# An attention, expert and mixer kernel: shared token differences, and unread matmuls beside batch 0's attention

## The chip, the cores and the metric

The kernel runs on one core of one Trainium2 chip. The metric is the device time of one execution in microseconds, the median of the runs. A core has TensorE (PE, matmuls), VectorE (DVE), ScalarE (ACT), GpSimd (POOL) and SyncE (SP, which here issues most DMAs), each with its own instruction stream executed in order.

## What is computed

Three stages, one after another, on 4 batches of 576 tokens with 512 channels (8 heads of 64):

```python
# attention, with a bias from a running sum of s
scores = scale * q @ k.T + min(-(cum[i] - cum[j]), 0), causal
x = softmax(scores) @ v                       # 4 x 576 x 512
# gated expert ("MoE"), with token mixtures
x_prev = x shifted by one token, zero first
xk = mu_k * x + (1 - mu_k) * x_prev
xr = mu_r * x + (1 - mu_r) * x_prev
y = sigmoid(xr @ w_r) * (relu(xk @ w_k) ** 2 @ w_v)
# mixer
u = y + (relu(y.T @ w_tok1) @ w_tok2).T
out = u + relu(u @ w_ch1) @ w_ch2
```

The weights arrive in 64-bit floats and are turned into pairs of 32-bit values (a high and a low part) on the chip; most products are then three matmuls (high by high, high by low, low by high).

## The kernel before

**Order.** The program is written with a tile framework: each piece of work is given a place (`at(x)`), a planner orders the instructions of each engine by place and by its own estimate of durations, and the semaphores follow from the tiles. An edit therefore can change the order of instructions that it doesn't touch. Buffers come from pools; a tile waits for the release of an older one of the same tag. `ps_d` has two PSUM buffers of tag `d`, used by the expert's products while attention runs.

**Batch 0's attention** is done in two parts. `early(h, j)` (L308) handles the first 256 tokens of head h in two blocks j of 128 queries: a score matmul in fp32 (L314), `softmax_max` (DVE, L258) and `softmax` (exponent on ACT, L268; sum and reciprocal on DVE, L269 and L270; scaling on POOL, L271), transposes on PE (L322), a copy by ACT, and the products with v (`pv`, L332). `late(h, j)` (L354) handles the remaining queries of head h in three blocks, j = 2, 3, 4 (the last of 64 queries), with scores at L364, transposes at L373, and `late_pv(h)` (L381, matmuls at L391) once per head; every second head the result is copied by DVE to `xt` (L393, by the helper at L77). Meanwhile the weights of the expert are loaded by SP (L553) and split by `weight_split` (ACT L75 and L565, DVE L566 and L567, then POOL or DVE L571). The buffers XK, XR and KK lie where the first weights' staging buffers were, so they can't be written before the last of these splits.

**The other batches** use `scores`, `transposes` and `values` (matmuls at L283, L284, L405, L457), 40 blocks per batch.

**The expert** works in chunks of 256 and 320 tokens (`CHS`), two per batch b. Its units (`moe_units`, L518) are laid out beside the attention blocks: per chunk eight `up` units (tile h, L482), then `gate` (tile r) and `down` (tile vd) units, twenty in all. `mix(b, c, i, p)` (L466) makes one 128-channel quarter p of XK (i = 0, read by `up`) or XR (i = 1, read by `gate`): on DVE a TENSOR_SCALAR by mu (L472) and a SCALAR_TENSOR_TENSOR by 1 - mu (L473), a rounding copy on ACT (L474), and the low part on DVE (L475). Its working tile has the tag t, of which there are three, shared with `up`'s. Where the mixtures are made is set at L533 to L540: XR for a first chunk beside its first `up` units, XK for the second chunk of batches 1 to 3 right after the eight `up` units of the first, XR for the second chunk beside the last four units of the first, XK for the next batch's first chunk beside the last units of this batch and the first of the next.

**The mixer** follows when attention is over, from about 500 us on; it is not touched.

The mask tile `maskc` (zeros, and a triangle of large negative values in its last 128 columns) and the identity are made on POOL in `constants` (L146).

Of the kernel before, what the change touches and what calls it, by code (L numbers as in the profile page):

```python
# [8 lines left out]
F32 = mybir.dt.float32  # L9
# [4 lines left out]
AF = mybir.ActivationFunctionType  # L14
ALU = mybir.AluOpType
# [4 lines left out]
def f32(ap):  # L20
    return ap.bitcast(F32)
# [3 lines left out]
def attention_moe_mixer(  # L25
# [16 lines left out]
    nc = tc.nc  # L42
    G, D, _, S = qk.shape
# [6 lines left out]
    KD = DM // 128  # L50
    KF = FF // 128
# [5 lines left out]
    CM = S - QC  # L57
# [6 lines left out]
    def open_pool(**kw):  # L64
        st = ExitStack()
        return st, st.enter_context(tc.tile_pool(**kw))

    def at(place):
        return tc.high_priority(tc.cur_priority - int(place * 1000))
# [3 lines left out]
    def copy(e, out, in_, scale=1.0):  # L73
        if e == "A":
            nc.scalar.activation(out=out, in_=in_, func=AF.Copy, scale=scale)  # L75
        elif e == "D" and scale == 1.0:
            nc.vector.tensor_copy(out, in_)  # L77
        else:
            ENG[e].tensor_scalar(out=out, in0=in_, scalar1=scale, scalar2=1.0, op0=ALU.mult, op1=ALU.mult)

    const = ctx.enter_context(tc.tile_pool(name="const", bufs=1, reuse_waits="tile"))
# [3 lines left out]
    ps_d = ctx.enter_context(tc.tile_pool(name="ps_d", bufs=2, space=PSUM, reuse_waits="tile"))  # L85

    ident = const.tile([128, 128], F32, name="ident")
    maskc = const.tile([128, 512 + 128], BF16, name="maskc")
    mu = const.tile([128, 2, KD], F32, name="mu")
    omu = const.tile([128, 2, KD], F32, name="omu")  # L90

    WK = wp.tile([128, 2 * KD * FF], F32R, name="WK")
    WV = wp.tile([128, 2 * KF * DM], F32R, name="WV")
# [4 lines left out]
    act = {"ps": ps_d}  # L98
# [37 lines left out]
    def pt_tile(slot, dtype=F32):  # L136
        return pt_p.tile([128, (NS - 1) * CM], dtype, tag=f"PT{slot}", name=f"PT{slot}")
# [6 lines left out]
    xt = {}  # L144

    def constants():  # L146
        nc.gpsimd.memset(maskc, 0.0)
        nc.gpsimd.affine_select(
            out=maskc[:, 512:640], in_=maskc[:, 512:640], pattern=[[-1, 128]],
            compare_op=ALU.is_ge, fill=-8.0e9, base=0, channel_multiplier=1,  # L150
        )
        make_identity(nc, ident)

    def mixes():
        for i, m in enumerate((mu_k, mu_r)):
            nc.scalar.dma_start(out=mu[:, i, :], in_=m.rearrange("(k p) -> p k", p=128))
        nc.vector.tensor_scalar(out=omu, in0=mu, scalar1=-1.0, scalar2=1.0, op0=ALU.mult, op1=ALU.add)

# [94 lines left out]
    def softmax_max(j, ps, P, mx, x, c0, c1):  # L255
        m = min(128, S - 128 * j)
        q0 = 128 * j
        nc.vector.tensor_tensor_reduce(  # L258
            out=P[0:m, c0:c1], in0=ps[0:m, 0:c1 - c0], in1=maskc[0:m, 512 - q0 + c0:512 - q0 + c1],
            scale=-scale, scalar=3.0e38 if x == 0 else mx[0:m, x - 1:x],  # L260
            op0=ALU.add, op1=ALU.min, accum_out=mx[0:m, x:x + 1],
        )
# [30 lines left out]
    def early_view(h):  # L293
        t, h0, n = next(x for x in early_at if x[1] <= h < x[1] + x[2])
        return t[:, 0:2 * n * QC].rearrange("p (h t s) -> p h t s", h=n, t=2), h0, n
# [12 lines left out]
    def early(h, j, V0, cp):  # L308
        x, h0, _ = early_view(h)
        w = 128 * j + 128  # L310
        P = cp.tile([128, w], F32, tag=f"E{j}", name=f"P{j}", bufs=2)
        mx = st_p.tile([128, 2], F32, tag="mx", name="mx")
        ps = ps_s.tile([128, 512], F32, tag="s", name="s")
        nc.tensor.matmul(ps[:, 0:w], x[0:D + 2, h - h0, 0, 128 * j:w], x[0:D + 2, h - h0, 1, 0:w], start=True, stop=True)  # L314
        softmax_max(j, ps, P, mx, 0, 0, w)
        softmax(j, P, mx, 0)
        if j == 0:
            pt[0] = ps_t.tile([128, 512], F32, tag="t", name="t")
        ps = pt[0]
        for k in range(j + 1):  # L320
            o = 128 * (j + k)
            nc.tensor.transpose(ps[:, o:o + 128], P[:, 128 * k:128 * k + 128], ident)  # L322
        if j == 0:
            return
        T = cp.tile([128, FIRST], F32, tag="T", name="T", bufs=2)
        copy("A", T, ps[:, 0:FIRST])
        if h % 2 == 0:
            early_ps[h // 2] = ps_v.tile([128, QC], F32, tag="v", name="pv")
        pv = early_ps[h // 2]
        r = slice(D * (h % 2), D * (h % 2) + D)  # L330
        for k in range(2):
            nc.tensor.matmul(pv[r, 128 * k:QC], V0[:, k, h * D:h * D + D], T[:, QC * k:QC + 128 * k], start=k == 0, stop=k == 1)  # L332
        if h % 2 == 1:
            x = xt[0, h // 2] = xt_p.tile([128, 1 + S], F32, tag="xt", name="xt")
            nc.gpsimd.memset(x[:, 0:1], 0.0)
            copy("D", x[:, 1:1 + QC], pv)
# [17 lines left out]
    def late(h, j):  # L354
        m = min(128, S - 128 * j)
        w = 128 * j + m
        q0 = 128 * j
        x = late_x.pop(h) if j == NS - 1 else late_x[h]
        P = p_p.tile([128, w], F32, tag=f"P{j}", name=f"P{j}")
        mx = st_p.tile([128, 2], F32, tag="mx", name="mx")  # L360
        parts = [(0, w)] if w <= 512 else [(0, w // 2), (w // 2, w)]
        for y, (c0, c1) in enumerate(parts):
            ps = ps_s.tile([128, 512], F32, tag="s", name="s")
            nc.tensor.matmul(ps[0:m, 0:c1 - c0], x[0:D + 4, 0, q0:q0 + m], x[0:D + 4, 1, c0:c1], start=True, stop=True)  # L364
            softmax_max(j, ps, P, mx, y, c0, c1)
        softmax(j, P, mx, y)
        if j == QC // 128:
            late_t[h] = pt_tile(h % 2)
        T = late_t[h]
        pt = ps_t.tile([128, 512], F32, tag="t", name="t")  # L370
        for k in range(j + 1):
            r = min(128, S - 128 * k)
            nc.tensor.transpose(pt[0:r, m * k:m * k + m], P[0:m, 128 * k:128 * k + r], ident[0:m, 0:m])  # L373
        o = q0 - QC
        nf = j + 1 if m == 128 else j
        view = T.rearrange("p (k w) -> p k w", w=CM)
        copy("A", view[:, 0:nf, o:o + m], pt[:, 0:m * nf].rearrange("p (k m) -> p k m", m=m))
        if nf <= j:
            copy("A", T[0:TAIL, BLK[j] + o:BLK[j] + o + m], pt[0:TAIL, m * j:m * j + m])
# [83 lines left out]
        nc.scalar.activation(out=tmp[a, 0:n], in_=ps[z, :], func=AF.Copy)  # L463
        nc.vector.tensor_tensor(out=x[a, 1 + base:1 + base + n], in0=ps[a, :], in1=tmp[a, 0:n], op=ALU.add)

    def mix(b, c, i, p):  # L466
        dst = act[("XK", "XR")[i]]
        x = xt[b, p]
        a, z = CHS[c]
        n = z - a  # L470
        t = act["sm"].tile([128, CM], F32, tag="t", name="t", bufs=3)
        nc.vector.tensor_scalar(out=t[:, 0:n], in0=x[:, 1 + a:1 + z], scalar1=mu[:, i, p:p + 1], scalar2=1.0, op0=ALU.mult, op1=ALU.mult)  # L472
        nc.vector.scalar_tensor_tensor(out=t[:, 0:n], in0=x[:, a:z], scalar=omu[:, i, p:p + 1], in1=t[:, 0:n], op0=ALU.mult, op1=ALU.add)  # L473
        nc.scalar.activation(out=dst[:, 0, p, 0:n], in_=t[:, 0:n], func=AF.Copy)  # L474
        nc.vector.tensor_tensor(out=dst[:, 1, p, 0:n], in0=t[:, 0:n], in1=f32(dst[:, 0, p, 0:n]), op=ALU.subtract)  # L475

    def up(b, c, m):
        n = width(c)
# [39 lines left out]
    def moe_units(b):  # L518
        u = []
        for c in range(2):  # L520
            for m in range(KF):
                u.append([(up, b, c, m)])
            seq = [("g", 0), ("g", 1)]
            for m in range(KD):
                seq += [("d", m)] + ([("g", m + 2)] if m + 2 < KD else [])
            for w, m in seq:
                if w == "g":
                    u.append([(gate, b, c, m)])
                else:
                    u.append([(down, b, c, m, 0)])  # L530
                    u.append([(down, b, c, m, 1)])
        n = len(u) // 2
        for p in range(KD):  # L533
            u[1 + p].append((mix, b, 0, 1, p))
            u[KF + 1 + p if b else n - KD + p].append((mix, b, 1, 0, p))
            u[n - KD + p].append((mix, b, 1, 1, p))
            if b + 1 < B and p < KD - 1:
                u[n + n - KD + p].append((mix, b + 1, 0, 0, p))
        if b:
            u[0].insert(0, (mix, b, 0, 0, KD - 1))  # L540
        return u

    def run(acts):
# [51 lines left out]
    def attention_item(n):  # L595
# [65 lines left out]
        with at(N0 + n + 2):  # L661
            if j == QC // 128 - 1:
                values(i, 0)
            if j == NS - 1:
                values(i, 1)

    wst_s, sp = open_pool(name="wst", bufs=5)
    cp_s, cp = open_pool(name="cp", bufs=1)
    cum, e32 = bias_rows(cp)
# [31 lines left out]
    with at(9):  # L701
        mixes()
# [5 lines left out]
    x = 1.0  # L708
# [16 lines left out]
    x = 18  # L725
# [5 lines left out]
            x += 1.5  # L731
    with at(N0):
        for p in range(KD):
            mix(0, 0, 0, p)
    todo = {}
    base = (NS - 2) * H
    starts, ends = [0, 2, 4, 4], [2, 4, 4, 4]
    for b in range(B):
        u = moe_units(b)
        x0 = base + NS * H * (b - 1) + starts[b] if b else 0  # L740
        x1 = base + NS * H * b + ends[b]
        if b == 0:
            x1 = base + NS * H + ends[0]
            u, u1 = u[:len(u) // 2], u[len(u) // 2:]
            for x, acts in enumerate(u1):
                m = base + 1
# [222 lines left out]
```

## Time and profile before

| | |
|---|---|
| three runs | 890.91, 886.45, 890.05 us; median 890.05 |
| profiled execution, whole | 893.86 us |
| its span, first to last instruction | 891.5 us |
| mean granted TensorE clock | 0.965 |
| busy: PE, DVE, ACT, POOL | 94%, 59%, 52%, 35% of the span |
| instructions | 17414 |

The span is that of the execution in which all instructions were recorded; 2.4 us of its time lie around the span. Busy time of PE is from the start of a matmul to its modelled end, so a busy PE need not be at its peak. The granted clock is given as a share of 2.4 GHz; 0.50 is 1.2 GHz.

### The profile page before, as it was taken

The page shows a single profiled execution, that of the slowest core. Times are in us where ns is not written, and L with a number is a line of the kernel's source. Part 1 is how long each engine was busy: PE and PEld are TensorE (multiplying, and loading weights), DVE is VectorE, ACT ScalarE, POOL GpSimd, SP SyncE. Part 2 cuts the span into 40 slices and gives each one's busy share as a digit, 9 for nine tenths or more (in the row PEclk, how much of TensorE's full clock was granted, in tenths as well). Part 3 has the DMA queues.
Part 4 walks back from the last instruction along what each step waited for, and adds up shares of the span by engine and source line. Part 5 has one row for each costly group of instructions (what it writes and reads, how often), then busy time and mean ns, then how long its engine had stood idle before and what let it go on. Part 6 is the DMA issues. An engine that isn't in the chain of part 4 may idle for free.

```text
span 891.5 us, 17414 instructions
## 1 busy us (share of the span) xinstructions
PE 842.4 (94%) x6008; PEld 778.0 (87%) x6008; DVE 523.7 (59%) x1582; ACT 467.3 (52%) x1320; POOL 316.3 (35%) x463
## 2 busy tenths in 40 slices
PE   6578999999889999998999899899999999999998
PEld 4234777998789999888999899899999999999998
DVE  5687786677979677887657866871331322322221
ACT  4685885966786867858546785760320211211210
POOL 4544444754664545645244774650000000000000
PEclk9657999999999999999999999999999999999999
DMA  7972345456646355532042656654021112112100
GB/s 183 202 213 57 99 125 121 109 138 135 155 101 138 82 115 136 128 98 48 20 130 74 189 174 193 208 164 148 25 70 58 46 42 60 43 43 65 43 24 25
DMA packets 74888, 94.19 MB, mean 106 GB/s; under 512 B 10304, under 2 KB 58432, under 8 KB 74800
## 3 DMA queue, kind: packets, MB, share of 16 engines
q1 hardware_dynamic: 68352, 77.40, 33.8%
q0 software_dynamic: 4576, 15.08, 5.5%
q8 instruction: 48, 0.79, 0.4%
q10 hardware_dynamic: 1872, 0.59, 0.3%
q14 instruction: 40, 0.33, 0.1%
HBM read 56.50 MB, written 14.75 MB: 80 GB/s over the span
## 4 chain that ended last, share of the span: by engine, by line
PE 75%; DVE 9%; DMA 6%; ACT 4%; issue 3%; POOL 2%; SPq 0%; ACTq 0%; DVEq 0%; POOLq 0%
PE c L109 32%; PE vd L109 10%; PE h L109 9%; PE r L109 5%; PE t L109 4%; PE pv L457 3%; PE t L405 3%; PE pv L391 2%; PE s L283 2%; PE s L364 2%; PE s L284 2%; DVE raw L566 2%; DMA raw<-in_moe_w_k_dram 2%; DVE raw L567 1%; DVE P L258 1%
## 5 line engine op out<-in xcount | busy, mean ns | idle before, releaser
L808 ACT ACTIVATE HID<-c 128x256 fp32r<-128x256 f32 (+1 forms) x96 | 39.4, 410 | 219.8 <-PE c L109 219.5
L271 POOL TENSOR_SCALAR P<-P,sum 64x576 f32<-64x576 f32 (+4 forms) x160 | 101.2, 637 | 124.4 <-DVE sum L270 55.2
L109 PE MATMUL h<-XK,WK 128*128 128x256 f32 (+1 forms) x768 | 123.8, 302 | 1.7 <-ACT k L484 1.1
L109 PE MATMUL vd<-KK,WV 128*128 128x256 f32 (+1 forms) x768 | 117.9, 298 | 0.6 <-DVE sum L269 0.3
L109 PEld LDWEIGHTS h<-XK,WK 128*128 128x128 f32 x768 | 107.0, 189 | 6.2 <-ACT k L484 1.5
L268 ACT ACTIVATE P<-P,mx 64x576 f32<-64x576 f32 (+4 forms) x160 | 95.7, 599 | 23.0 <-DVE mx L258 21.1
L109 PEld LDWEIGHTS vd<-KK,WV 128*128 128x128 f32 x768 | 105.5, 188 | 2.4 <-DVE e L515 0.7
L109 PE MATMUL c<-U,WK 128*128 128x256 f32 (+1 forms) x768 | 104.2, 294 | 2.2 <-DVE HID L809 2.2
L109 PE MATMUL c<-HID,WV 128*128 128x256 f32 (+1 forms) x768 | 104.4, 291 | 0.0
L109 PEld LDWEIGHTS c<-U,WK 128*128 128x128 f32 x768 | 100.2, 190 | 2.5 <-DVE HID L809 2.5
L109 PEld LDWEIGHTS c<-HID,WV 128*128 128x128 f32 x768 | 100.4, 188 | 0.0
L809 DVE SCALAR_TENSOR_TENSOR HID<-c,HID 128x256 fp32r<-128x256 f32 (+1 forms) x96 | 43.8, 457 | 84.1 <-ACT HID L808 84.1
L258 DVE CUSTOM_DVE_ANT_0 P<-s,maskc 64x288 f32<-64x288 f32 (+4 forms) x160 | 74.7, 473 | 20.0 <-PE s L284 4.9
L873 DVE TENSOR_TENSOR ut<-c,ut 128x256 f32<-128x256 f32 (+1 forms) x32 | 14.7, 458 | 119.5 <-PE c L109 108.5
L566 DVE SCALAR_TENSOR_TENSOR raw<-raw 128x256 int32<-128x256 int32 (+2 forms) x85 | 51.2, 604 | 29.9 <-ACT raw L565 27.1
L75 ACT ACTIVATE raw<-raw 128x256 f32<-128x256 f32 (+2 forms) x101 | 46.9, 465 | 34.5 <-DMA raw<-in_moe_w_ch_dram 10.8
L487 POOL TENSOR_TENSOR KK<-k,KK 128x256 fp32r<-128x256 f32 (+1 forms) x64 | 54.2, 850 | 26.2 <-ACT k L486 25.7
L109 PE MATMUL r<-XR,WR 128*128 128x320 f32 (+1 forms) x384 | 61.1, 298 | 0.0
L567 DVE SCALAR_TENSOR_TENSOR raw<-raw 128x256 int32<-128x256 int32 (+2 forms) x85 | 54.0, 638 | 1.3
L109 PE MATMUL c<-HID,WR 128*128 128x256 f32 (+1 forms) x384 | 54.5, 291 | 0.0
L109 PEld LDWEIGHTS r<-XR,WR 128*128 128x128 f32 x384 | 53.2, 188 | 0.9
L405 PE MATMUL t<-ident,P 128*128 128x128 f32 (+1 forms) x360 | 52.2, 263 | 1.5 <-DVE PT L434 0.7
(111 smaller groups left out, 1618.1 us busy)
## 6 DMA issues: line engine op xcount, KB each, us to landing
X<-HL SPq DMA_DIRECT2D x72, 288.0 KB
raw<-in_moe_w_ch_dram POOLq DMA_DIRECT2D x48, 256.0 KB, 3.6
qkr<-in_qk_dram SPq DMA_DIRECT2D x48, 144.0 KB
yt<-y_d SPq DMA_DIRECT2D x16, 288.0 KB
u_d<-yt SPq DMA_DIRECT2D x16, 288.0 KB
raw<-in_moe_w_k_dram SPq DMA_DIRECT2D x8, 512.0 KB
raw<-in_moe_w_v_dram SPq DMA_DIRECT2D x16, 256.0 KB
ut<-u_d SPq DMA_DIRECT2D x32, 128.0 KB
```

Of the source, the lines that this page charges most:

```text
L75: nc.scalar.activation(out=out, in_=in_, func=AF.Copy, scale=scale)
L109: nc.tensor.matmul(ps, a, b, start=first and i == 0, stop=last and i == n - 1)
L258: nc.vector.tensor_tensor_reduce(out=P[0:m, c0:c1], in0=ps[0:m, 0:c1 - c0], in1=maskc[0:m, 512 - q0 + c0:512 - q0 + c1], scale=-scale, sca ...
L268: nc.scalar.activation(out=P[0:m, 0:w], in_=P[0:m, 0:w], func=AF.Exp, bias=mx[0:m, x:x + 1], scale=-1.0, accum_out=sm[0:m, 0:1])
L271: nc.gpsimd.tensor_scalar(out=P[0:m, 0:w], in0=P[0:m, 0:w], scalar1=sm[0:m, 1:2], scalar2=1.0, op0=ALU.mult, op1=ALU.mult)
L405: nc.tensor.transpose(ps[0:r, p0 + m * k:p0 + m * k + m], P[0:m, 128 * k:128 * k + r], ident[0:m, 0:m])
L457: nc.tensor.matmul(ps[:, o:n], vv[:, k, :], part, start=(k == 0 and t == 0), stop=(k == nk - 1 and t == len(parts) - 1),)
L487: nc.gpsimd.tensor_tensor(out=kk[:, 1, m, 0:n], in0=t[:, 0:n], in1=f32(kk[:, 0, m, 0:n]), op=ALU.subtract)
L566: nc.vector.scalar_tensor_tensor(out=low, in0=high, scalar=3, in1=low, op0=ALU.logical_shift_left, op1=ALU.bitwise_or)
L567: nc.vector.scalar_tensor_tensor(out=low, in0=high, scalar=-2 ** 31, in1=low, op0=ALU.bitwise_and, op1=ALU.bitwise_or)
L808: nc.scalar.activation(out=hi, in_=ps, func=AF.Relu)
L809: nc.vector.scalar_tensor_tensor(out=lo, in0=ps, scalar=0.0, in1=f32(hi), op0=ALU.max, op1=ALU.subtract)
```

## The change

Two things are changed.

The mixtures are computed as x0 + mu (x - x0), where x0 is the previous token. The difference `d` is one TENSOR_TENSOR on DVE, and each mixture one SCALAR_TENSOR_TENSOR from it, with the ACT copy and the low part as before. `mix` makes both XK and XR of a quarter from one `d`, except in batch 0's first chunk, where the two are still made apart (XK before the first unit, XR beside the first `up` units). XK for the second chunk is now made beside the last four units of the first chunk for all batches, and XR for the next batch's first chunk together with its XK. The tile 1 - mu goes.

`keep_busy(n, x, w)` issues n matmuls on PE with x as both operands and w columns; they all write to one PSUM tile `idle`, which nothing reads, and which holds one of the two buffers of tag `d` from the start until its last write. Thirteen of them (bf16, 512 columns, on the zeros of the mask) stand at the front of the program, four follow the transposes of every `early` block (fp32, 128 columns, on P), and three follow those of `late` blocks j = 2 and 3 of heads 0 to 2. The zeros of the mask are written by DVE, ahead of everything, and no longer by POOL.

```diff
     def constants():
-        nc.gpsimd.memset(maskc, 0.0)
         nc.gpsimd.affine_select(
...
+    def keep_busy(n, x, w):
+        for _ in range(n):
+            nc.tensor.matmul(act["idle"][:, 0:w], x[:, 0:128], x[:, 0:w], start=True, stop=True)
+
     def mixes():
...
-        nc.vector.tensor_scalar(out=omu, in0=mu, scalar1=-1.0, scalar2=1.0, op0=ALU.mult, op1=ALU.add)
...
             nc.tensor.transpose(ps[:, o:o + 128], P[:, 128 * k:128 * k + 128], ident)
+        keep_busy(4, P, 128)
         if j == 0:
...
             nc.tensor.transpose(pt[0:r, m * k:m * k + m], P[0:m, 128 * k:128 * k + r], ident[0:m, 0:m])
+        if h < 3 and m == 128:
+            keep_busy(3, P, 128)
...
-    def mix(b, c, i, p):
-        dst = act[("XK", "XR")[i]]
+    def mix(b, c, p, which=(0, 1)):
         x = xt[b, p]
         a, z = CHS[c]
         n = z - a
-        t = act["sm"].tile([128, CM], F32, tag="t", name="t", bufs=3)
-        nc.vector.tensor_scalar(out=t[:, 0:n], in0=x[:, 1 + a:1 + z], scalar1=mu[:, i, p:p + 1], scalar2=1.0, op0=ALU.mult, op1=ALU.mult)
-        nc.vector.scalar_tensor_tensor(out=t[:, 0:n], in0=x[:, a:z], scalar=omu[:, i, p:p + 1], in1=t[:, 0:n], op0=ALU.mult, op1=ALU.add)
-        nc.scalar.activation(out=dst[:, 0, p, 0:n], in_=t[:, 0:n], func=AF.Copy)
-        nc.vector.tensor_tensor(out=dst[:, 1, p, 0:n], in0=t[:, 0:n], in1=f32(dst[:, 0, p, 0:n]), op=ALU.subtract)
+        d = act["sm"].tile([128, CM], F32, tag="t", name="d", bufs=3)
+        nc.vector.tensor_tensor(out=d[:, 0:n], in0=x[:, 1 + a:1 + z], in1=x[:, a:z], op=ALU.subtract)
+        for i in which:
+            dst = act[("XK", "XR")[i]]
+            t = act["sm"].tile([128, CM], F32, tag="t", name="t", bufs=3)
+            nc.vector.scalar_tensor_tensor(out=t[:, 0:n], in0=d[:, 0:n], scalar=mu[:, i, p:p + 1], in1=x[:, a:z], op0=ALU.mult, op1=ALU.add)
+            nc.scalar.activation(out=dst[:, 0, p, 0:n], in_=t[:, 0:n], func=AF.Copy)
+            nc.vector.tensor_tensor(out=dst[:, 1, p, 0:n], in0=t[:, 0:n], in1=f32(dst[:, 0, p, 0:n]), op=ALU.subtract)
...
         for p in range(KD):
-            u[1 + p].append((mix, b, 0, 1, p))
-            u[KF + 1 + p if b else n - KD + p].append((mix, b, 1, 0, p))
-            u[n - KD + p].append((mix, b, 1, 1, p))
+            if b == 0:
+                u[1 + p].append((mix, 0, 0, p, (1,)))
+            u[n - KD + p].append((mix, b, 1, p))
             if b + 1 < B and p < KD - 1:
-                u[n + n - KD + p].append((mix, b + 1, 0, 0, p))
+                u[n + n - KD + p].append((mix, b + 1, 0, p))
         if b:
-            u[0].insert(0, (mix, b, 0, 0, KD - 1))
+            u[0].insert(0, (mix, b, 0, KD - 1))
...
+    nc.vector.memset(maskc, 0.0)
+    act["idle"] = ps_d.tile([128, 512], F32, tag="d", name="idle")
+    keep_busy(13, maskc, 512)
     wst_s, sp = open_pool(name="wst", bufs=5)
...
         for p in range(KD):
-            mix(0, 0, 0, p)
+            mix(0, 0, p, (0,))
```

## Rows read from the trace of the kernel before

**Rows 1.** The page: TensorE's granted clock in 40 slices, in tenths.
```profile
PEclk9657999999999999999999999999999999999999
```
**Rows 2.** Windows: stretch, its length, busy us (instructions) of each engine, clock, DMA.
```profile
core 0: us, PE busy (x) PEld busy (x) DVE busy (x) ACT busy (x) POOL busy (x), PEclk, DMA share, GB/s
...
18.00:40.00 22.00, 12.00 (x46) 6.67 (x46) 14.35 (x51) 14.77 (x38) 13.39 (x17) 0.71 0.92 194
28.00:68.00 40.00, 27.66 (x60) 11.46 (x61) 30.34 (x70) 28.80 (x68) 21.96 (x23) 0.50 0.79 194
40.00:48.00 8.00, 8.00 (x16) 3.29 (x15) 3.41 (x12) 4.01 (x11) 1.93 (x3) 0.50 0.92 292
48.00:76.00 28.00, 19.39 (x53) 8.22 (x52) 27.14 (x55) 21.92 (x54) 15.66 (x14) 0.56 0.49 133
...
72.00:82.00 10.00, 8.58 (x20) 3.80 (x21) 4.77 (x16) 6.91 (x20) 3.25 (x4) 0.50 0.33 85
84.00:500.00 416.00, 402.14 (x2933) 370.06 (x2932) 319.62 (x1082) 298.18 (x864) 212.99 (x303) 0.99 0.45 109
```
**Rows 3.** Windows of 2 us, where the clock rises and falls; same columns.
```profile
68.00:70.00 2.00, 2.00 (x12) 1.06 (x11) 1.97 (x3) 0.44 (x1) 2.00 (x2) 0.90 0.00 0
70.00:72.00 2.00, 0.42 (x4) 0.18 (x2) 1.97 (x4) 0.33 (x1) 1.08 (x1) 0.95 0.00 0
```
**Rows 4.** Timeline of PE: start, us, group, [idle time before, releaser].
```profile
6.78 4.47 PE L314 MATMUL s<-HL 66*128 66x128 f32 x12 [6.78 <-DMA HL<-in_qk_dram]
...
13.63 1.54 PE L332 MATMUL pv<-T,V 128*64 128x256 f32 x4
...
17.22 0.86 PE L332 MATMUL pv<-T,V 128*64 128x256 f32 x4
...
38.75 4.48 PE L364 MATMUL s<-X 68*128 68x384 f32 x6 [4.43 <-DMA VV<-in_v_dram]
...
64.62 4.25 PE L391 MATMUL pv<-PT,VV 128*64 128x320 f32 x10
...
69.44 0.98 PE L373 MATMUL t<-ident,P 128*128 128x128 f32 x7
72.47 1.22 PE L364 MATMUL s<-X 68*64 68x288 f32 x2 [2.05 <-DVE mx L258]
...
75.36 1.65 PE L364 MATMUL s<-X 68*128 68x384 f32 x2 [0.95 <-DVE mx L258]
...
83.72 0.49 PE L373 MATMUL t<-ident,P 128*128 128x128 f32 x3
...
87.39 0.81 PE L364 MATMUL s<-X 68*128 68x384 f32 x2
```
**Rows 5.** Timeline of DVE, same columns.
```profile
40.40 0.56 DVE L258 CUSTOM_DVE_ANT_0 P<-s,maskc 128x384 f32<-128x384 f32 x1 [3.03 <-PE s L364]
...
81.48 0.49 DVE L77 COPY xt<-pv 128x320 f32<-128x320 f32 x1 [4.92 <-PE pv L391]
81.89 1.09 DVE L475 TENSOR_TENSOR XK<-t,XK 128x256 fp32r<-128x256 f32 x3
```
**Rows 6.** The chain that ended last, in order of time: start, us, what.
```profile
77.01 4.44 PE pv L391 x10
...
89.58 2.74 PE h L109 x24
...
93.19 2.34 PE pv L391 x10
```
**Rows 7.** Instructions of a line: duration in ns, min/median/max, first and last start.
```profile
L472 DVE TENSOR_SCALAR t<-xt,mu x64: 334/377/2569, 54.9 to 491.3; 128x256 f32<-128x256 f32 x32, 128x320 f32<-128x320 f32 x32
...
L475 DVE TENSOR_TENSOR XK<-t,XK x32: 395/473/1849, 81.9 to 488.3; 128x256 fp32r<-128x256 f32 x16, 128x320 fp32r<-128x320 f32 x16
```
**Rows 8.** PE's waits, 84 to 500 us: us in total, times, longest.
```profile
PE pv L457 <- DVE xt L464: 6.2, 4, 2.5
```
**Rows 9.** Timeline of all engines at the seam near 398 us.
```profile
398.24 0.31 PE L109 MATMUL h<-XK,WK 128*128 128x320 f32 x1
...
398.64 0.49 DVE L475 TENSOR_TENSOR XR<-t,XR 128x320 fp32r<-128x320 f32 x1
```

More of the change, by code (lines that the diff above doesn't have):

```diff
@@ L89, in attention_moe_mixer @@
     mu = const.tile([128, 2, KD], F32, name="mu")
-    omu = const.tile([128, 2, KD], F32, name="omu")
     WK = wp.tile([128, 2 * KD * FF], F32R, name="WK")
```

## The prediction

> **What bounds the kernel now.** I read the granted clock by slices first, then busy times by stretch, then the chain of work that ended last, then the timelines of TensorE (PE) and VectorE (DVE) where that chain changes engines. There are two regimes. From 84 us on PE sets the time: between 84 and 500 us it is busy 402.1 of 416 us [rows 2], and the reader is to see that nothing off PE counts there except through the 13.9 us that PE stands idle. Before 84 us PE does not set the time. It idles 10.0 of the 22 us from 18 to 40, and from 48 to 76 DVE is busy 27.1 of 28 us, mostly with weight splits [rows 2]. That is the only stage where the clock is low [rows 1]: 0.50 from 28 to 68 and from 72 to 82 us [rows 2, 3]. The columns give 1.00 from 0 us, but durations say otherwise: the same four pv records take 1.54 us at 13.63 and 0.86 us at 17.22 [rows 4], so until about 17 us PE too was at its lower level (1.2 GHz), and the 1.00 is only what stood there before the first recorded change.
>
> At the end of that stage the slow clock lies on the path. The first expert matmuls (h, 83.4 us) need XK; the XK subtraction stands on DVE at 81.89, right behind the copy of xt, which waited 4.92 us for pv [rows 5]; pv is 4.44 us of PE in the chain at 77.01 and 2.34 us for the same ten records at 93.19 [rows 6]. So the whole PE-bound remainder starts as late as this slow piece lets it, and what is gained or lost by 84 us is gained or lost at the end.
>
> **Price of an unread matmul.** One head's pv is ten records of 320, 320, 320, 192 and 64 columns, two each (an fp32 matmul leaves two records): 2432 record columns, so 0.96 ns each at full clock and 1.83 at half [rows 6]. An added 128 by 128 fp32 matmul is 256 of them: 0.25 us at full clock, 0.47 at half. The thirteen at the front are one-pass, 512 wide: 24 h matmuls of 256 columns take 2.74 us [rows 6], 0.45 ns a column, so 13 x 512 columns are 3.0 us at full clock and 5.7 at half (by the 1.90 of pv).
>
> **Part 1, the thirteen at the front.** They follow a DVE memset at about 1 us and end by 4 to 6.7 us; the first score starts at 6.78 because its q and k only land then [rows 4]. PE was idle before it, so they cost nothing (bounds 0 to +1), and they should let the scores start at full clock. That itself gains nothing at the end, since the stage behind it waits for other things.
>
> **Part 2, four after each early block, 16 blocks.** 64 x 0.25 = 15.7 us at full clock, 30 at half. Cover: the 10.0 us of PE idle between 18 and 40 [rows 2], and about 5 us given back between 6.78 and 17 by running at full clock what ran at half. So 0 at full clock, bounds 0 to +6. What queues behind them on PE are the next head's scores, and DVE's maxima behind those.
>
> **Part 3, three after each of two blocks of late heads 0 to 2.** 18 matmuls. Head 0's fall near 50 us, in the stretch 38.75 to 52 where PE runs its first late scores without a break at half clock [rows 4]. Head 1's six follow the transposes at 69.44; PE is idle 2.05 us before 72.47 [rows 4], and 6 x 0.25 = 1.5 us fits in there. Head 2's six follow the transposes at 83.72 [rows 4] and those of its next block a microsecond later, where PE is full: 6 x 0.25 = **+1.5 us** on the path. They also hold one of the two PSUM buffers that h uses, until about 85 us, when one h has run: nothing (0 to +1).
>
> **Part 4, what the clock gives.** The clock fell in 70 to 72, just where PE had its 2.05 us gap [rows 3, 4]; head 1's six fill three quarters of it. I take it that the clock then holds to 82. On the chain this is 4.44 - 2.34 = 2.1 us for pv and 1.65 - 0.81 = 0.8 us for the scores ahead of it (75.36 against 87.39 [rows 4]): **-2.9 us** (0 to -2.9). Earlier, from 40 to 48, DVE is busy only 3.4 of 8 us [rows 2]: 3.03 us it waited up to 40.40 for a score that itself ran at half clock [rows 5], the rest mostly for ScalarE (ACT) and data. With scores at full speed it could draw maxima and sums of head 0 and head 1, some 2.5 us of work, out of the full stretch 48 to 76: **-2.5 us** (0 to -4.6, all the idle time).
>
> By the Trainium skill (TensorE: Matmul & The Clock Gate, Terms) the penalty of a throttled clock is the throttled time times one minus the clock ratio. Taken over this trace it would be a far larger gain, the fourth rival below; the chain speaks against it, since most of that time ends in waits for DVE and DMA. [...]
>
> **Part 5, the mixtures.** 64 TENSOR_SCALAR go (median 377 ns) and 36 TENSOR_TENSOR come: 28 shared by both outputs, 8 in batch 0's first chunk, where the two mixtures stay apart. A subtraction of two SBUF tensors of the same size is 473 ns [rows 7]. DVE is relieved of 64 x 0.377 - 36 x 0.473 = 7 us in medians; long ones (to 2.57 us) go too, so up to 15. ACT's copies are the same in number. PE's share: it idles 13.9 us between 84 and 500 [rows 2], of which 6.2 us is pv waiting for DVE's xt [rows 8]. I take **-3 us** (+1 to -6), about half of that wait.
>
> **Part 6, what is moved.** XK for the second chunk of batches 1 to 3 is made seven units later, and XR for the next batch's first chunk four or five earlier, both at the seam between chunks. There h starts at 398.24 while the last XR subtraction runs at 398.64 [rows 9], so a K made in the same pair comes just in time or up to 0.9 us late. Six seams; DVE's queue behind holds maxima, and PE's holds the next attention block. I take **+1 us** (0 to +5.4). The three buffers of tag t, one of them now d, let only two mixtures stand ready instead of three before XK may be written; the third follows in the time of head 1's pv (0 to +1). The memset of the mask moves from POOL to DVE, idle then: nothing.
>
> **Sum.** -2.9 - 2.5 + 1.5 - 3 + 1 = -5.9 us. The profiled execution took 893.86 us, so 888.0 by its own time; the median of the runs is 3.8 us lower, and the same difference makes 890.05 - 5.9 = **884.1 us**. About 0.5%, or 4.5 us, is what a measurement of this kernel can tell from no change: faster is under 885.6, slower over 894.5.
>
> **Rivals.**
> *The clock doesn't hold.* Head 1's six are too little, or the planner's order leaves a longer gap; both gains of part 4 vanish: 890.05 - 0.5 = 889.5. For it: PE was unbroken from 38.75 to 52 and stayed at 0.50, so work alone was not enough there. Against: the ten pv records at 64.62 did bring it up, in 68 to 70 [rows 3, 4].
> *The unread matmuls crowd PE (slower).* If the early heads run at half clock, the 64 are 30 us against 10.0 of idle, and late scores slip by 20 us. The stretch 48 to 76 has 8.6 us of PE idle [rows 2]; from a slip over that on, the rest, 11.4 us, is path: 889.5 + 11.4 = 901. Against: the clock stands at full from 17 to 26 us without them.
> *The seams stall.* The K subtraction of the last quarter gets three R operations before it, 1.6 us by six seams, 9.6 in place of 1: 884.1 + 8.6 = 892.7. For it: DVE is full there. Against: PE's products take that quarter last.
> *Everything at half clock counts.* PE is busy 27.7 us in 28 to 68 and 8.6 in 72 to 82 [rows 2]; half of 36.2 is 18.1 in place of 5.4: 871.4. Against: DVE's 27.1 of 28 us.
>
> **How the numbers follow.** Forecast 0.50 (880 to 889), clock not held 0.22, crowding 0.09, seams 0.11, half-clock time 0.08. Range 876 to 895: it leaves out crowding and the half-clock case, and the tail of the seams, 0.19 in all. Faster: 0.36 of the forecast, 0.08, and 0.04 of the unheld clock, 0.48. Same: 0.14 + 0.17 + 0.06 = 0.37. Slower: 0.09 + 0.05 + 0.01 = 0.15.
>
> **What would show it.** Right: four pv records near 0.86 us before 15 us; ten pv records at about 2.3 us before 84 us; the first h at 78 to 79.5 us; PE's idle after 84 us lower, its wait for xt too; 18 late unread matmuls near 0.25 us. Wrong: half clock in 72 to 82; first late score after 45 us; h waiting for XK at the seams.

## The result, and the profile after

The changed kernel is slower: 900.73 us, the median of six runs (895.04 to 903.74), against 890.12 us for six runs of the kernel before (886.45 to 893.20). The ratio is 1.0103, with a 95% interval of 1.0072 to 1.0134, so about 9 us lost (6 to 12; the two medians alone are 10.6 apart). The forecast was a gain of 6 us; the sign was wrong, and the time lies above the range.

The profiled execution took 902.53 us. From its page, busy time of PE and the granted clock in 40 slices:

```profile
span 900.8 us, 17748 instructions
...
PE 860.3 (96%) x6185; PEld 799.5 (89%) x6185; DVE 520.0 (58%) x1554; ACT 469.8 (52%) x1320; POOL 312.5 (35%) x462
...
PEclk8978999989899999999999999999999999999999
```

The 6 and 5 of the second and third slices in [rows 1] are 9 and 7 now; the 8 of the ninth slice, from 180 us on, is new. The same stretches as in [rows 2], and the one around 185 us (columns as there):

```profile
18.00:40.00 22.00, 21.84 (x151) 17.63 (x150) 17.90 (x61) 17.87 (x45) 14.43 (x17) 1.00 0.98 278
28.00:68.00 40.00, 33.24 (x188) 22.31 (x186) 38.05 (x93) 32.92 (x80) 28.36 (x28) 0.87 0.69 180
40.00:48.00 8.00, 8.00 (x50) 5.36 (x47) 7.35 (x22) 8.00 (x22) 5.56 (x6) 1.00 1.10 267
48.00:76.00 28.00, 19.50 (x81) 10.48 (x80) 24.99 (x57) 21.13 (x55) 13.91 (x13) 0.74 0.38 104
72.00:82.00 10.00, 9.76 (x32) 5.06 (x33) 4.69 (x21) 5.22 (x17) 1.99 (x3) 0.66 0.22 60
84.00:500.00 416.00, 399.99 (x2882) 365.68 (x2882) 307.77 (x1038) 295.19 (x849) 207.67 (x302) 0.98 0.45 107
180.00:190.00 10.00, 9.34 (x45) 8.73 (x46) 6.85 (x28) 6.14 (x18) 2.23 (x4) 0.66 0.57 123
```

In the early stage PE gained. The clock is 0.87 instead of 0.50 from 28 to 68 us, and DVE does 7.35 us of work from 40 to 48 where it did 3.41 [rows 2]. The timeline of PE in that stage (start, duration, group, idle time before and its releaser):

```profile
1.26 5.73 PE L154 MATMUL idle<-maskc 128*128 128x512 bf16 x13 [1.26 <-DVE maskc L673]
...
10.75 2.93 PE L315 MATMUL s<-HL 66*128 66x256 f32 x8 [2.63 <-DVE mx L259]
...
14.24 1.91 PE L154 MATMUL idle<-P 128*128 128x128 f32 x8
...
19.92 0.86 PE L334 MATMUL pv<-T,V 128*64 128x256 f32 x4
...
23.01 1.05 PE L154 MATMUL idle<-P 128*128 128x128 f32 x8
...
34.55 0.91 PE L366 MATMUL s<-X 68*128 68x384 f32 x2
...
68.55 0.38 PE L108 MATMUL h<-XK,WK 128*128 128x256 f32 x1
...
72.24 1.65 PE L366 MATMUL s<-X 68*128 68x384 f32 x2 [1.89 <-DVE mx L259]
73.82 4.51 PE L395 MATMUL pv<-PT,VV 128*64 128x320 f32 x10
...
81.08 0.83 PE L154 MATMUL idle<-P 128*128 128x128 f32 x6
```

The first late score runs at 34.55 instead of 38.75 us [rows 4], the first h at 68.55 instead of 83.4. What that is worth is seen further on, where both kernels do the same work. A view of all PE instructions gives these starts, in us, of the first matmul of each of the expert's eight chunks (tile h) and of the mixer (tile c):

| chunk | 1 | 2 | 3 | 4 | 5 | 6 | 7 | 8 | mixer |
|---|---|---|---|---|---|---|---|---|---|
| before | 83.4 | 145.1 | 212.9 | 289.6 | 346.6 | 398.2 | 453.7 | 493.3 | 552.7 |
| after | 68.5 | 143.6 | 218.9 | 290.6 | 353.6 | 405.6 | 459.4 | 498.8 | 560.1 |
| after - before | -14.9 | -1.5 | +6.0 | +1.0 | +7.0 | +7.4 | +5.7 | +5.5 | +7.4 |

So 14.9 us at the first h are 1.5 us by the second chunk, and the loss comes after that, between 145 and 560 us. (Single landmarks sway by some us, since the order within a batch differs; the trend is what counts.) What PE waited for between 84 and 500 us (us in total, times, longest), to be held against [rows 8]:

```profile
PE s L284 <- DVE mx L259: 4.0, 7, 1.8
PE pv L461 <- DVE PT L438: 2.8, 3, 1.7
PE pv L461 <- DVE xt L468: 1.7, 2, 1.3
```

Before, PE's waits for the maxima and for the low parts of P were shorter:

```profile
PE s L283 <- DVE mx L258: 1.0, 3, 0.6
PE pv L457 <- DVE PT L434: 0.8, 1, 0.8
```

The wait for xt went from 6.2 to 1.7 us as forecast, but scores now wait for DVE's maxima, and pv for DVE's low parts of P: 4.0 and 2.8 us in place of 1.0 and 0.8. The longest of these waits, on DVE, POOL and PE around 178 us:

```profile
177.28 0.73 POOL L241 TENSOR_TENSOR VV<-VS,VV 128x256 fp32r<-128x256 f32 x1
177.35 2.73 DVE L479 SCALAR_TENSOR_TENSOR t<-d,mu,xt 128x256 f32<-128x256 f32 x1
177.97 0.87 POOL L493 TENSOR_TENSOR KK<-k,KK 128x320 fp32r<-128x320 f32 x1
178.81 0.98 POOL L241 TENSOR_TENSOR VV<-VS,VV 128x384 fp32r<-128x384 f32 x1
...
180.00 0.54 DVE L259 CUSTOM_DVE_ANT_0 P<-s,maskc 128x384 f32<-128x384 f32 x1
...
180.61 0.34 PE L284 MATMUL s<-X 128*64 128x288 f32 x1 [1.82 <-DVE mx L259]
```

One mixture stood on DVE for 2.73 us, the maximum of a score behind it came late, PE stood idle 1.82 us, and then ran at half clock: 0.66 in the window from 180 to 190 us, above.

### The profile page after: what moved, and what is told of

It reads as the page before. It is cut to its first block, busy times and chain, and to the rows that moved or that the text cites. A ratio compares the mean times of both kernels' runs of the same rounds, so it can differ in the third digit from the quotient of the medians.

```text
span 900.8 us, 17748 instructions
## 1 busy us (share of the span) xinstructions
PE 860.3 (96%) x6185; PEld 799.5 (89%) x6185; DVE 520.0 (58%) x1554; ACT 469.8 (52%) x1320; POOL 312.5 (35%) x462
## 4 chain that ended last, share of the span: by engine, by line
PE 71%; DVE 9%; DMA 9%; ACT 5%; issue 3%; POOL 2%; SPq 0%; ACTq 0%; DVEq 0%; POOLq 0%
PE c L108 32%; PE h L108 8%; PE vd L108 7%; PE r L108 4%; PE pv L461 3%; PE t L108 3%; DMA raw<-in_moe_w_ch_dram 3%; PE t L409 3%; DMA X<-HL 3%; PE pv L395 2%; PE s L366 2%; PE s L284 2%; DVE P L259 2%; PE s L285 1%; PE idle L154 1%
## 5 line engine op out<-in xcount | busy, mean ns | idle before, releaser
L108 PE MATMUL vd<-KK,WV 128*128 128x256 f32 (+1 forms) x768 | 124.4, 303 | 0.0
L269 ACT ACTIVATE P<-P,mx 64x576 f32<-64x576 f32 (+4 forms) x160 | 95.6, 598 | 31.7 <-DVE mx L259 28.4
L108 PEld LDWEIGHTS vd<-KK,WV 128*128 128x128 f32 x768 | 108.9, 191 | 2.2 <-DVE XR L481 0.4
L572 DVE SCALAR_TENSOR_TENSOR raw<-raw 128x256 int32<-128x256 int32 (+2 forms) x85 | 50.4, 594 | 33.4 <-ACT raw L571 31.4
L493 POOL TENSOR_TENSOR KK<-k,KK 128x256 fp32r<-128x256 f32 (+1 forms) x64 | 52.2, 818 | 28.4 <-ACT k L492 25.4
L573 DVE SCALAR_TENSOR_TENSOR raw<-raw 128x256 int32<-128x256 int32 (+2 forms) x85 | 52.5, 618 | 1.2
```

The costliest lines, as they stand in the source:

```text
L108: nc.tensor.matmul(ps, a, b, start=first and i == 0, stop=last and i == n - 1)
L269: nc.scalar.activation(out=P[0:m, 0:w], in_=P[0:m, 0:w], func=AF.Exp, bias=mx[0:m, x:x + 1], scale=-1.0, accum_out=sm[0:m, 0:1])
L493: nc.gpsimd.tensor_tensor(out=kk[:, 1, m, 0:n], in0=t[:, 0:n], in1=f32(kk[:, 0, m, 0:n]), op=ALU.subtract)
L572: nc.vector.scalar_tensor_tensor(out=low, in0=high, scalar=3, in1=low, op0=ALU.logical_shift_left, op1=ALU.bitwise_or)
L573: nc.vector.scalar_tensor_tensor(out=low, in0=high, scalar=-2 ** 31, in1=low, op0=ALU.bitwise_and, op1=ALU.bitwise_or)
```

## The experiments

Four theories were weighed. A: the mixtures cost it, by their operands (64 TENSOR_SCALAR with one SBUF operand become instructions with two) or by their new places. B: the unread matmuls cost it, on PE. C: any edit redraws the planner's order, and this draw is a bad one. D, which came up only after the first four runs: the three buffers of tag t. `mix` now takes one for d and one for each of its two mixtures, which is all three; so the next difference, and the relu of the next `up` unit, which takes the same tag (L483 before, L489 after), must wait until XK and XR of the quarter are done. All kernels compute the whole reference. The figures are medians, and the ratio with its interval to the kernel before, which ran again beside each of three groups. Its medians there were 891.71 us (beside the halves, the formula and the places), 892.47 us (beside the two kernels in place, the thirteen at the front alone, and the places with the unread matmuls) and 890.87 us (beside the rest). Kernels of different groups are therefore compared by their ratios, in us of 890.

**One half each.** The first takes `keep_busy` out of the changed kernel and puts the memset back on POOL; the second adds all unread matmuls to the kernel before.

```diff
 (against the changed kernel)
+        nc.gpsimd.memset(maskc, 0.0)
...
-    nc.vector.memset(maskc, 0.0)
-    act["idle"] = ps_d.tile([128, 512], F32, tag="d", name="idle")
-    keep_busy(13, maskc, 512)
...
-        keep_busy(4, P, 128)
...
-        if h < 3 and m == 128:
-            keep_busy(3, P, 128)
```

> The mixtures of the change (shared difference, both outputs at one place), without any unread matmul and with the mask's zeros on POOL as before. Theory A (the loss lies in the mixtures: DVE instructions with two SBUF operands stretched while POOL works, the maxima behind them late, PE idle, the clock falling after it, as at 177 us of the changed kernel): 897 to 902 us. Theory B (the unread matmuls are paid on PE): 885 to 891. Theory C (the planner's new order scatters stalls, whatever the edit): anything from 888 to 900, with stalls at other places than those of the changed kernel.

Measured: 898.98 us, 1.0070 (1.0046 to 1.0095).

> All the unread matmuls and the mask on DVE, with the mixtures of before. Theory A: 886 to 890, ahead by some 2.5 us at 100 us as in the changed kernel, and nothing lost after. Theory B: 897 to 901, lost before 100 us. Theory C: 888 to 900, lost after 150 us at places without a mixture.

Measured: 889.36 us, 0.9975 (0.9947 to 1.0003). So most of the loss, or all of it, is the mixtures', and B falls: the unread matmuls alone cost nothing that can be measured. In their trace the clock held at 1.00 from 72 to 82 us, and the ten pv records at 72.53 took 2.34 us.

**The mixtures taken apart.** The new formula at the old places, each mixture with a difference of its own, in one buffer; and the old formula at the new places:

```diff
 (formula, against the kernel before)
-        nc.vector.tensor_scalar(out=t[:, 0:n], in0=x[:, 1 + a:1 + z], scalar1=mu[:, i, p:p + 1], scalar2=1.0, op0=ALU.mult, op1=ALU.mult)
-        nc.vector.scalar_tensor_tensor(out=t[:, 0:n], in0=x[:, a:z], scalar=omu[:, i, p:p + 1], in1=t[:, 0:n], op0=ALU.mult, op1=ALU.add)
+        nc.vector.tensor_tensor(out=t[:, 0:n], in0=x[:, 1 + a:1 + z], in1=x[:, a:z], op=ALU.subtract)
+        nc.vector.scalar_tensor_tensor(out=t[:, 0:n], in0=t[:, 0:n], scalar=mu[:, i, p:p + 1], in1=x[:, a:z], op0=ALU.mult, op1=ALU.add)
 (places, against the kernel before)
-            u[1 + p].append((mix, b, 0, 1, p))
-            u[KF + 1 + p if b else n - KD + p].append((mix, b, 1, 0, p))
-            u[n - KD + p].append((mix, b, 1, 1, p))
+            if b == 0:
+                u[1 + p].append((mix, 0, 0, 1, p))
+            u[n - KD + p] += [(mix, b, 1, 0, p), (mix, b, 1, 1, p)]
...
-                u[n + n - KD + p].append((mix, b + 1, 0, 0, p))
+                u[n + n - KD + p] += [(mix, b + 1, 0, 0, p), (mix, b + 1, 0, 1, p)]
...
-            u[0].insert(0, (mix, b, 0, 0, KD - 1))
+            u[0][0:0] = [(mix, b, 0, 0, KD - 1), (mix, b, 0, 1, KD - 1)]
```

> The kernel before with only the formula changed: each mixture by its own difference (64 TENSOR_TENSOR in place of 64 TENSOR_SCALAR), at the places of before, nothing shared. Theory A in the form that the operand count matters: slower, 893 to 900, with more stretched mixtures. Theory A in the form that the places matter: 889 to 893. Theory B: 890. Theory C: 886 to 898.

Measured: 894.91 us, 1.0033 (1.0008 to 1.0057).

> The kernel before with only the places changed: the old formula, keys' and gate's mixtures made at the places of the change. Theory A in the form that the places matter (two mixtures together hold DVE just where the softmax needs it): 895 to 902. In the form that operands matter: 889 to 893. Theory B: 890. Theory C: 886 to 898.

Measured: 890.30 us, 0.9981 (0.9955 to 1.0007). The places cost nothing, the operands some 3 us with all 64 differences made (the change makes 36). Neither is the loss of 9. What the change has and neither of these two has is the third buffer held by d.

**One line: the last mixture over d.** Each quarter then takes two buffers instead of three. It was made to the mixtures alone and to the whole change:

```diff
-            t = act["sm"].tile([128, CM], F32, tag="t", name="t", bufs=3)
+            t = d if i == which[-1] else act["sm"].tile([128, CM], F32, tag="t", name="t", bufs=3)
```

> The mixtures of the change alone, but the last mixture of a quarter is written over the difference, so that a pair needs two of the three buffers of tag t and no longer all three. Theory D (the three buffers are the cause: a pair takes them all, the next pair and the relu of the next h wait, and what stands behind them on DVE and ACT waits too): 887 to 892 us, as with the places alone (890.3). Theory C (the planner's order for these mixtures is worse whatever the buffers): 894 to 900.

Measured: 887.19 us, 0.9941 (0.9913 to 0.9969).

> The whole change with that one line: the unread matmuls too. Theory D: 885 to 890, the mixtures alone less the 2.4 us that the unread matmuls gave by themselves. Theory C: 893 to 902.

Measured: 889.23 us, 0.9959 (0.9939 to 0.9979). By the ratios the line gives back 11.5 us in the one and 12.8 in the other, and turns both from slower into faster than before. Without it (mixtures alone, 314 to 320 us), the timeline of DVE, with two rows of POOL's:

```profile
314.60 1.00 POOL L238 TENSOR_TENSOR VV<-VS,VV 128x384 fp32r<-128x384 f32 x1
314.72 1.17 DVE L469 TENSOR_TENSOR d<-xt 128x256 f32<-128x256 f32 x1
315.99 0.73 DVE L473 SCALAR_TENSOR_TENSOR t<-d,mu,xt 128x256 f32<-128x256 f32 x1
...
317.61 0.88 POOL L487 TENSOR_TENSOR KK<-k,KK 128x320 fp32r<-128x320 f32 x1 [1.16 <-ACT k L486]
317.66 1.11 DVE L475 TENSOR_TENSOR XK<-t,XK 128x256 fp32r<-128x256 f32 x1
318.80 0.48 DVE L473 SCALAR_TENSOR_TENSOR t<-d,mu,xt 128x256 f32<-128x256 f32 x1
319.20 0.28 DVE L256 CUSTOM_DVE_ANT_0 P<-s,maskc 128x128 f32<-128x128 f32 x1
...
319.42 0.14 DVE L267 TENSOR_SCALAR sum<-sum 64x1 f32<-64x1 f32 x1
```

and of PE in the same kernel:

```profile
319.55 0.50 PE L281 MATMUL s<-X 128*128 128x512 f32 x1 [1.07 <-DVE sum L267]
```

With the line, the same quarter of the same chunk:

```profile
313.36 0.52 DVE L469 TENSOR_TENSOR d<-xt 128x256 f32<-128x256 f32 x1
...
315.07 0.54 DVE L473 SCALAR_TENSOR_TENSOR t<-d,mu,xt 128x256 f32<-128x256 f32 x1
...
317.06 1.24 DVE L473 SCALAR_TENSOR_TENSOR d<-d,mu,xt 128x256 f32<-128x256 f32 x1
318.22 0.41 DVE L475 TENSOR_TENSOR XK<-t,XK 128x256 fp32r<-128x256 f32 x1
```

Without it two buffers hold d and XK's mixture, and the third still holds the relu of the last `up` (tile k), which POOL reads until 318.49. The second mixture (318.80) comes only after XK's low part, which ends at 318.77, has freed a buffer. Behind it stands the maximum (319.20) that frees the PSUM tile for PE's next score, and PE is idle for 1.07 us. (The row names the sum that began at 319.42, as the maximum ended; in the program a score waits for no sum.) With the line both mixtures are made before XK's low part, and the longest idle time that PE's rows show from 310 to 322 us is 0.30 us.

**Buffers taken away and added.** If the cause is the count of buffers and not something else in that line, then the harmless change of places must become slow with two buffers, and the mixtures must recover with four. A fourth fits in SBUF only if the mixer gives up one of its five yt buffers, so a control has four yt and three t.

```diff
 (against the places alone; both tiles of tag t)
-        t = act["sm"].tile([128, CM], F32, tag="t", name="t", bufs=3)
+        t = act["sm"].tile([128, CM], F32, tag="t", name="t", bufs=2)
 (control, against the mixtures alone)
-            t = mx_p.tile([128, S], F32, tag="yt", name="yt", bufs=5)
+            t = mx_p.tile([128, S], F32, tag="yt", name="yt", bufs=4)
 (against the control; all three tiles of tag t)
-        d = act["sm"].tile([128, CM], F32, tag="t", name="d", bufs=3)
+        d = act["sm"].tile([128, CM], F32, tag="t", name="d", bufs=4)
```

> The mirror of the in-place run: the old formula at the new places (890.3 us with three buffers of tag t), but with two buffers of tag t, so that a pair of mixtures takes them all. Theory D (a pair that takes all buffers stalls the rest): 896 to 903 us, idle time of TensorE up by 6 or more us. Theory C (any edit draws a new order): no direction, 886 to 899.

Measured: 898.18 us, 1.0076 (1.0052 to 1.0100), by the ratios 8.5 us over the same kernel with three. The idle time of PE was not up by 6 us: over the whole span it is 45.4 us against 48.5, and 4.9 us more in the stretch of the table below.

> A control for the next one: the mixtures of the change alone, three buffers of tag t, and four buffers of tag yt of the mixer in place of five, to make room. If yt's fifth buffer matters little: 897 to 900, as with five (899.0). If it is needed: up to 905.

Measured: 898.71 us, 1.0080 (1.0052 to 1.0107), as the mixtures alone.

> The control with a fourth buffer of tag t and nothing else changed. Theory D: 6 to 12 us faster than the control, 886 to 893. Theory C: no more than 4 us from the control either way. If it was only that the difference should not outlive the pair (operands, places) and not the count: as the control.

Measured: 889.98 us, 0.9988 (0.9966 to 1.0011), 8.7 us under its control. Four pairs of kernels that differ by one buffer of tag t, in what a quarter takes or in what there is, show 8 to 13 us each by the ratios, in the same direction; D is shown, and C as the whole story falls, since four separate draws would hardly agree so. PE's busy time and its matmuls from 145 to 580 us, one row for each kernel from the view of stretches:

| kernel | busy, us | matmuls |
|---|---|---|
| after | 413.8 | 2996 |
| mixtures alone | 411.3 | 2989 |
| control, four yt | 412.3 | 2983 |
| places, two buffers | 413.3 | 2990 |
| before | 414.7 | 3027 |
| after, in place | 417.1 | 3038 |
| mixtures alone, in place | 419.5 | 3026 |
| four buffers | 417.4 | 3044 |
| places, three buffers | 418.2 | 3039 |
| unread matmuls alone | 413.6 | 3041 |
| places and unread matmuls | 419.4 | 3073 |
| formula alone | 413.3 | 3004 |

The four with a buffer too few do 2983 to 2996 matmuls in those 435 us, the five after them 3026 to 3044: 30 to 60 fewer, at 435 / 3030 = 0.144 us each some 4 to 9 us. The busy time alone doesn't set the four apart from the rest (the kernel before has 414.7), but each of them is busy 3 to 8 us less than its partner with a buffer more. The formula alone lies between, as its time does. (Places and unread matmuls together are the last experiment below.)

**The unread matmuls in parts, and with the places.** The first has the thirteen at the front alone, the second the four after each early block alone, the third adds all of them to the old formula at the new places.

```diff
 (front, against the kernel before)
-        nc.gpsimd.memset(maskc, 0.0)
...
+    nc.vector.memset(maskc, 0.0)
+    act["idle"] = ps_d.tile([128, 512], F32, tag="d", name="idle")
+    keep_busy(13, maskc, 512)
 (early, against the front alone)
+        keep_busy(4, P, 128)
...
-    keep_busy(13, maskc, 512)
```

> Of the unread matmuls only the thirteen at the front, old mixtures. If the front ones bring the gain (the early scores at full clock): 888 to 890, clock up before 10 us. If the ones beside the blocks bring it: 891 to 893, clock down from 10 us on and from some 27 to 68 us as before. A first score that is late by up to 1 us: nothing at the end.

Measured: 891.62 us, 0.9989 (0.9965 to 1.0012).

> Of the unread matmuls only the four after each early block, old mixtures, mask's zeros on DVE. If these bring the 2.4 us that all the unread ones gave: 887 to 890, clock full from 17 to some 50 us. If the late ones or the whole set are needed: 891 to 893. If they crowd TensorE: 894 or more, and the first late score after 45 us.

Measured: 888.78 us, 0.9979 (0.9957 to 1.0001).

> The old formula at the new places, with the unread matmuls: the two parts that did no harm alone. If gains add: 886 to 889. If the order of the middle is a lottery that every edit draws again (theory C): 886 to 899.

Measured: 882.87 us, 0.9882 (0.9845 to 0.9919), on four runs, the fastest of all and below both expectations: by the ratios 10.5 us below the kernel before, and 2.2% of its time below the change. It keeps the TENSOR_SCALAR, three buffers with one for each mixture, and takes the unread matmuls. Neither part shows more than 0.25% alone, so here a gain beyond their sum appears, and what makes it was not taken apart. On the mixtures in place the same matmuls gave nothing (0.9941 without, 0.9959 with). The late unread matmuls alone were not tried, nor four t buffers beside five yt.

## Why the prediction was wrong

**The step that failed** is the last but one sentence of part 6: that three buffers of tag t, one of them now d, let only two mixtures stand ready, "0 to +1". It saw the shortage and priced it once, at batch 0's start, where the mixtures wait for the staging buffers. But the same three buffers serve all 28 pairs, and the relu of `up` besides, for 400 us in which PE has next to no slack (13.9 us of 416 [rows 2]). The runs show 8 to 13 us for it in place of 0 to 1, 12.8 in the changed kernel itself. With that size the sum is -5.9 + 12.8, a loss of 7 us where 9 (6 to 12) were measured; without the shortage the change measured 0.9959, a gain of 3.7 us where the rest of the sum says 5.9. That this rest comes out so near is in part luck, since its terms did not come as forecast (below).

The Trainium skill (Perfetto Trace Analysis, Identifying Performance Opportunities) says that gaps recurring on the engine that should be saturated can mean that there is no room to allocate the next tile, by the count of buffers. The traces agree so far as PE's waits for DVE's maxima come seven times in the changed kernel, 4.0 us, where they came three times, 1.0 us; the wait for a buffer has no row of its own.

How the cost arises is only partly separated: the planner knows of the buffers and lays its order by them, so the steps of DVE at 314 to 320 us are partly an order written before the run and partly waiting in it. No run held the order fixed while it changed the count. Nor is it the same in each pair where the time goes. From 145 to 580 us PE's waits for maxima and sums add up to 5.6 us in the changed kernel and 2.0 with the line, but to 4.1 and 4.2 in the mixtures alone without and with it. The granted clock in that stretch is 0.98 in the changed kernel and 0.99 with the line, but 0.98 in the mixtures alone either way.

**Part 1** held for the most part: the thirteen took 5.73 us and ended at 7.0, just past the 4 to 6.7 forecast, and alone they change nothing (0.9989). The first scores did start at full clock, 0.20 us a record at 6.95 as at 25.01:

```profile
6.95 1.18 PE L315 MATMUL s<-HL 66*128 66x128 f32 x6
...
25.01 0.39 PE L315 MATMUL s<-X 66*128 66x128 f32 x2
```

It did not last: PE idled 2.63 us ahead of 10.75, and at 14.24 eight unread records took 1.91 us against 1.05 at 23.01. So the 5 us that part 2 expected back between 6.78 and 17 did not come in that stretch, and the first early pv ran at 19.92 us, not before 15.

**Part 2** held in its result. The four matmuls after an early block add 1.05 us at full clock (0.98 forecast), PE from 18 to 40 us went from 12.0 to 21.8 busy of 22, and the late scores came 4.2 us earlier, not later. The rival of crowding fell with it: matmuls alone 0.9975, early ones alone 0.9979. That its 901 us lies beside the measured 900.73 is chance.

**Part 3** was near enough: the three matmuls after a late block (six records) took 0.83 us at 81.08, so two such groups take 1.7 us, against the +1.5 for head 2's.

**Part 4** failed in this kernel, and its remedy is not what decides. The gap ahead of the scores at 72 us is still there, 1.89 us where it was 2.05 [rows 4], the clock fell, and pv took 4.51 us, no less than before [rows 6]. Head 1's six did not fill the gap: both groups, at 66.23 and 67.34, had ended by 68.2, and the gap began at 70.35. In DVE's queue the split of a weight that had only just landed stood ahead of that maximum:

```profile
71.15 0.43 DVE L572 SCALAR_TENSOR_TENSOR raw<-raw 128x256 int32<-128x256 int32 x1 [1.79 <-ACT raw L571]
71.49 0.68 DVE L259 CUSTOM_DVE_ANT_0 P<-s,maskc 128x512 f32<-128x512 f32 x1
```

Where DVE's order had no such gap, the whole change in place, the clock held. Its stretch and its pv:

```profile
72.00:82.00 10.00, 10.00 (x60) 6.81 (x60) 6.60 (x24) 6.68 (x22) 3.44 (x4) 1.00 0.39 115
```

```profile
74.71 2.41 PE L395 MATMUL pv<-PT,VV 128*64 128x320 f32 x10
```

That is the 2.1 us of the sum. But the early unread matmuls alone, with none behind the late blocks, show the same, so the late ones were not needed for it:

```profile
72.00:82.00 10.00, 10.00 (x58) 6.44 (x59) 6.55 (x24) 7.02 (x20) 1.99 (x3) 1.00 0.31 90
```

```profile
74.48 2.41 PE L395 MATMUL pv<-PT,VV 128*64 128x320 f32 x10
```

The step behind the other 2.5 came too, in the changed kernel itself: DVE drew work into 40 to 48 us. But the step from there to the end was too confident. The claim that "what is gained or lost by 84 us is gained or lost at the end" used the first h as the mark; it moved by 14.9 us and the second chunk by 1.5, since the first h was only pulled ahead of attention work that PE had to do anyway. With the unread matmuls alone, the last head's pv of batch 0 came at 141.00 instead of 146.80 us, 5.8 us earlier and close to the forecast; of that the whole time shows 2.2 us by the ratio and at most 4.7 by its interval. The second chunk begins 5.0 us earlier in that kernel (140.1 us) and the fourth 2.0 (287.6); why it goes back was not traced.

**Part 5** was right about DVE and wrong about what it is worth. In the grouping by line, the subtractions and mixtures and their low parts together take 95.6 us (38.3 + 21.0 + 19.0 + 17.3) where they took 104.8 (36.5 + 34.1 + 17.7 + 16.5), a relief of 9 us within the 7 to 15 forecast, and PE's wait for xt fell by 4.5 us. The groups of the difference and of the mixture (ns, min/median/max):

```profile
L475 DVE TENSOR_TENSOR d<-xt x36: 394/478/1166, 52.6 to 495.7; 128x256 f32<-128x256 f32 x20, 128x320 f32<-128x320 f32 x16
...
L479 DVE SCALAR_TENSOR_TENSOR t<-d,mu,xt x64: 457/538/2729, 55.2 to 498.7; 128x256 f32<-128x256 f32 x32, 128x320 f32<-128x320 f32 x32
```

The difference at 478 ns is the 473 of [rows 7]. But PE's idle time from 84 to 500 us, which was to fall, rose from 13.9 [rows 2] to 16.0 us: waits for DVE's maxima and low parts of P took the place of those for xt. Whether the relief shows without the shortage of buffers is open. The mixtures in place alone are 0.9941, 5 us, against the 2 that parts 5 and 6 sum to, but with a fourth buffer in its place they are 0.9988, 1 us, and what sets the two apart was not looked into (the four yt are not it: 1.0080 against 1.0070).

**The rivals.** "The clock doesn't hold" happened, and gives 889.5 with nothing else. "The seams stall" had the right sign, but from a wrong cause, three R operations ahead of a K at six seams: the places alone, which bring that order, are 0.9981, and in the changed kernel the expert's matmuls waited 1.3 us in all for XK (1.0 for ACT's part, 0.3 for DVE's). The case that all half-clock time counts got nothing: in the whole change in place the clock rose from 0.50 to 0.83 in 28 to 68 us and to 1.00 in 72 to 82, and its time fell by 0.4%.

## What to carry over

When an edit adds a tile to a rotating set of buffers, count what one round of the loop holds against the count of buffers, at every round and for every other user of the tag, before counting instructions: one buffer too few cost more here than the whole gain that was forecast. A temporary whose last reader is the instruction that makes the next one can be written in place. And a gain in an early stage is read at a mark where both kernels have done the same work, not at the first instruction of the next stage.

## What the runs showed of the hardware

A mixture with two SBUF operands took 2.73 us where its median is 0.54, while POOL ran three instructions back to back from 177.28 to 179.79; it ended 0.29 us after the last of them. The Trainium skill (SBUF — State Buffer, SBUF: two separate sides) says that a DVE instruction with two SBUF inputs and a POOL instruction that reads SBUF exclude each other for a whole instruction. The trace agrees, and adds that DVE lost to three in a row. In the kernel with the mixtures alone the difference at 314.72 and XK's low part at 317.66, 1.17 and 1.11 us long, end likewise 0.29 and 0.28 us after a POOL instruction (from 314.60 to 315.60, and from 317.61 to 318.49).

The clock fell after an idle time of PE of 1.82 us at 180 us, with 0.66 granted over the next ten, though PE was busy for 9.34 of them. Before, PE was busy for all of 40 to 48 us with late scores at 0.50 [rows 2]; after, those that began at 34.55 ran at full clock from their start, behind the unread matmuls.
